# TensorE's opening: ten idle matmuls become 100 small ones in 64x64 quadrants and five of the old kind

## The chip, the cores and the metric

The kernel runs on one core of one Trainium2 chip. The metric is device time in microseconds for one launch, which takes `q`, `k`, `v`, `moe_w_in` and `moe_w_out` in float32 and returns one float32 array.

The engines that matter are TensorE (PE, with its weight loads shown apart as PEld), VectorE (DVE), ScalarE (ACT), GpSimd (POOL) and the sync engine (SP). DMA transfers are issued from the queues of POOL, SP and ACT.

## The reference

Windowed attention, then a feed-forward layer with a squared ReLU:

```python
# q, k, v: (8, 8, 576, 64); window = 32, dilation = 4
scores = scale * np.matmul(q, k.transpose(0, 1, 3, 2))
mask_plain = (rel >= 0) & (rel < window)                                   # heads 0 to 3
mask_dil = (rel >= 0) & (rel < window * dilation) & (rel % dilation == 0)  # heads 4 to 7
attn = softmax(np.where(masks, scores, -1e9))
x = np.matmul(attn, v).transpose(0, 2, 1, 3).reshape(4608, 512)
out = np.square(np.maximum(x @ w_in, 0.0)) @ w_out                         # w_in 512 x 2048, w_out 2048 x 512
```

## The kernel before, in words

The 4608 tokens pass through the feed-forward layer in tiles of 256 or 512 tokens. Each tile first multiplies by `w_in` (line 937, 16 blocks of the hidden dimension times four slices of the model dimension), then ACT evicts with a ReLU (line 950), DVE squares (line 951), and a second series of matmuls multiplies by `w_out` (line 979). The attention of the eight batches is woven between these matmuls, and its results go to `xT`, the moving operand of line 937. Every engine executes its own list of instructions in order. The order is written out by hand: a string, `PROGRAM`, holds short codes, and its first stretch (up to the first `|`) is what happens before the first feed-forward group.

That first stretch is called the head here. It does batch 0's attention:

- `load_qk` (line 171) and `load_v` (lines 192 and 198) issue, from POOL's queue, the transfers of `q`, `k` and `v` from HBM into staging tiles (`qb`, `kb`, `vd`, `vbd`). The same queue then issues `w_in` (line 1050) and `w_out` (line 1055).
- Codes `T` (line 761) transpose `q` and `k` on TensorE, as 64x64 or 80x64 pieces, into a PSUM tile `pa`; codes `C` (lines 768 to 776) copy them out.
- Codes `B` (line 791) put a mask's bias into PSUM, `S` (line 813) adds the scores in 64x64 quadrants, `E` (line 821) takes the exponential, `P` and `D` (lines 851 and 867) multiply by `v` and by ones, and `L`, `X` and `M` (lines 874, 877 and 884) divide.
- Codes `w` and `W` call `turn` (line 731): so many matmuls of a zero tile `idle` against itself. Their result is used by nobody. `w10` in front of the first transposes is ten of them with 512 columns; later `w1` and `W1` (256 columns) stand single between the steps. They write the PSUM tile `po`.

The tile `idle` is a part of `kbd` and is set to zero by a DVE memset (line 1001), which the first idle matmul waits for.

The PSUM pools of `po` and `pd` have one buffer each. Apart from idle matmuls their first users in the head are the `P` and `D` steps of heads 4 and 5 (code `P20`, at 12.18 us in the profile).

```python
PROGRAM = "... L1:q00123 z y L1:v0dp L1:q10123 w10 T00 C00a T10 C10a B00 B10 w1 S00 E00 ..."
```

## Time and profile before

| what | value |
|---|---|
| time, median of 3 | 299.54 us (299.31 to 303.17) |
| the profiled execution's own time | 299.32 us |
| its span, first to last instruction | 297.5 us |
| PE busy | 290.4 us, 3159 matmuls |
| ACT busy | 192.0 us |
| DVE busy | 168.0 us |
| POOL busy | 127.6 us |
| bytes moved by DMA | 35.37 MB |

The span ends 1.8 us short of the execution's own time; that rest lies outside the program's instructions. Times in the profile are counted from the span's start. A matmul's end is modelled, since matmuls overlap in the array: how fast TensorE goes is read from the distance between two starts. "Idle before" is the time in which an engine did nothing ahead of an instruction, with what ended it.

### The profile page before, as it was taken

How to read it: one execution, taken by the hardware profiler on the slowest of the kernel's cores; microseconds unless marked ns; L12 is line 12 of the kernel's file. 1: busy time of each engine (PE TensorE's matmuls, PEld its weight loads, DVE VectorE, ACT ScalarE, POOL GpSimd, SP SyncE). 2: the span in 40 equal slices, each digit the busy share in tenths (PEclk: the TensorE clock that was granted, in tenths of full speed). 3: DMA queues.
4: the chain of work that ended last, by engine and by line, in shares of the span. 5: the costliest groups of instructions: out<-in, count | busy, mean ns of one | idle time of the engine just before them, and what ended most of it. 6: DMA issues, size and time to landing. Idle time of an engine off the chain costs nothing.

```text
span 297.5 us, 7852 instructions
## 1 busy us (share of the span) xinstructions
PE 290.4 (98%) x3159; PEld 166.3 (56%) x3159; DVE 168.0 (56%) x508; ACT 192.0 (65%) x397; POOL 127.6 (43%) x208
## 2 busy tenths in 40 slices
PE   7899999999999999999999999999999999999994
PEld 3589657868755554555455445545554555445443
DVE  2776566967868665686749474957445234004400
ACT  6888568757958665888667667766676567127411
POOL 8579882676584383955783688100000000000000
PEclk9999999999999999999999999999999999999999
DMA  8999999999989999999999499112101200121022
GB/s 126 197 183 215 203 157 223 186 151 169 193 114 185 184 121 190 153 125 175 159 191 151 65 160 186 13 37 73 35 2 36 74 35 0 35 73 35 0 56 88
DMA packets 83124, 35.37 MB, mean 119 GB/s; under 512 B 52624, under 2 KB 78480, under 8 KB 83088
## 3 DMA queue, kind: packets, MB, share of 16 engines
q0 software_dynamic: 48992, 18.40, 54.8%
q1 hardware_dynamic: 33952, 16.38, 27.7%
q8 instruction: 25, 0.41, 0.6%
q10 hardware_dynamic: 144, 0.10, 0.1%
q14 instruction: 11, 0.09, 0.1%
HBM read 37.31 MB, written 9.44 MB: 157 GB/s over the span
## 4 chain that ended last, share of the span: by engine, by line
PE 90%; DMA 5%; ACT 2%; POOL 1%; issue 1%; DVE 1%; ACTq 0%; POOLq 0%
PE pf L937 42%; PE pf L979 40%; DMA w_in<-in_moe_w_in_dram 3%; DMA kb<-in_k_dram 2%; PE po L661 2%; PE pa L661 1%; PE pf L661 1%; POOL qb L171 1%; PE pa L277 1%; PE pd L661 1%; ACT rec L684 0%; ACT pt L698 0%; POOL kb L171 0%; ACT rec L674 0%; PE po L414 0%
## 5 line engine op out<-in xcount | busy, mean ns | idle before, releaser
L937 PE MATMUL pf<-xT,w_in 128*128 128x512 bf16 (+1 forms) x704 | 128.3, 341 | 1.3 <-DMA w_in<-in_moe_w_in_dram 1.3
L979 PE MATMUL pf<-w_out_sb,h2T 128*128 128x512 bf16 (+2 forms) x592 | 129.3, 374 | 0.0
L937 PEld LDWEIGHTS <-w_in 128*128 128x128 bf16 x704 | 77.9, 113 | 48.0 <-DMA w_in<-in_moe_w_in_dram 1.7
L950 ACT ACTIVATE h2T<-pf 128x512 bf16<-128x512 f32 x144 | 83.7, 600 | 29.5 <-PE pf L937 29.3
L951 DVE TENSOR_TENSOR h2T<-h2T 128x512 bf16<-128x512 bf16 x144 | 60.3, 424 | 60.1 <-ACT h2T L950 57.8
L979 PEld LDWEIGHTS <-h2T 128*128 128x128 bf16 x592 | 55.5, 98 | 61.6
L478 POOL DMA_DIRECT2D vbd<-in_v_dram x80 | 43.0, 547 | 24.3 <-DMA qb<-in_q_dram 10.2
L985 ACT COPY osb<-pf 128x512 f32<-128x512 f32 (+1 forms) x34 | 19.5, 573 | 49.7 <-PE pf L979 49.5
L171 POOL DMA_DIRECT2D qb<-in_q_dram x18 | 13.0, 720 | 9.7 <-DMA xx<-qb 7.9
L684 ACT ACTIVATE rec<-rec 128x576 f32<-128x576 f32 x24 | 16.4, 682 | 0.7
L698 ACT ACTIVATE pt<-pa 128x384 bf16<-128x384 f32 (+1 forms) x28 | 12.7, 498 | 6.2 <-DVE xT L689 3.7
L192 POOL DMA_DIRECT2D vbd<-in_v_dram x16 | 10.9, 691 | 9.1 <-DMA kb<-in_k_dram 4.3
L687 DVE TENSOR_TENSOR xT<-po,rec 128x512 bf16<-128x512 f32 x14 | 9.7, 691 | 7.5 <-ACT rec L684 7.2
L171 POOL DMA_DIRECT2D kb<-in_k_dram x18 | 12.7, 706 | 1.7 <-issue 0.7
L465 POOL DMA_DIRECT2D vd<-in_v_dram x20 | 12.0, 616 | 2.9 <-DMA vbd<-in_v_dram 2.9
L470 POOL DMA_DIRECT2D vbd<-in_v_dram x20 | 12.0, 615 | 2.7 <-DMA vbd<-in_v_dram 2.2
L700 DVE TENSOR_TENSOR pt<-pt,mask_n 128x448 bf16<-128x448 bf16 (+1 forms) x20 | 7.1, 373 | 9.5 <-ACT pt L698 9.4
L700 DVE TENSOR_TENSOR pt<-pt,mask_f 128x384 bf16<-128x384 bf16 x24 | 8.4, 355 | 6.0 <-ACT pt L698 5.9
L687 DVE TENSOR_TENSOR xT<-pf,rec 128x512 bf16<-128x512 f32 x10 | 6.9, 691 | 8.5 <-ACT rec L684 8.5
L492 DVE COPY qT<-xx 64x576 bf16<-64x576 bf16 (+1 forms) x30 | 10.8, 360 | 0.6
L661 PEld LDWEIGHTS <-vbd 64*64 64x64 bf16 x288 | 7.6, 107 | 4.2 <-issue 4.2
L698 ACT ACTIVATE pt<-pf 128x448 bf16<-128x448 f32 (+1 forms) x18 | 8.5, 521 | 0.5 <-PE pf L661 0.3
(156 smaller groups left out, 311.8 us busy)
## 6 DMA issues: line engine op xcount, KB each, us to landing
qb<-in_q_dram POOLq DMA_DIRECT2D x7, 320.0 KB, 5.3
kb<-in_k_dram POOLq DMA_DIRECT2D x7, 320.0 KB
vd<-in_v_dram POOLq DMA_DIRECT2D x32, 64.0 KB, 6.1
w_in<-in_moe_w_in_dram POOLq DMA_DIRECT2D x4, 512.0 KB, 8.6
w_out_sb<-in_moe_w_out_dram POOLq DMA_DIRECT2D x4, 512.0 KB, 13.0
out_dram<-osb SPq DMA_DIRECT2D x16, 128.0 KB, 5.3
qb<-in_q_dram POOLq DMA_DIRECT2D x7, 256.0 KB, 7.6
kb<-in_k_dram POOLq DMA_DIRECT2D x7, 256.0 KB
```

The source lines that it names most:

```text
L171: nc.gpsimd.dma_start(t[0:n, part, hs, :], src[b, hs, t0 : t0 + RES * n, :].rearrange("h (p r) d -> p h (r d)", r=RES))
L478: nc.gpsimd.dma_start(v_rows[b % 2][p0 + 16 * r : p0 + 16 * r + 16, e, :, :], v[b, 2 * e + hl, :, :].rearrange("(i m r) d -> r m i d", r=R ...
L661: nc.tensor.matmul(out, lhs, rhs, start=begin, stop=True, skip_group_check=True)
L684: nc.scalar.activation(rec[:, :], rec[:, :], ACT.Exp, scale=-1.0)
L687: nc.vector.tensor_tensor(out=tok[:, :, 16:M], in0=byr(o[:, :]), in1=byr(rec[:, 0:512]), op=ALU.mult)
L698: nc.scalar.activation(pt, sp[b, e][g][:, 0:n], ACT.Exp, scale=SCALE)
L700: nc.vector.tensor_tensor(out=pt, in0=pt, in1=mask, op=ALU.mult)
L937: nc.tensor.matmul(to, w_in_sb[piece][:, kt, c0 : c0 + 509 : 4], rhs, start=(kt == kts[0] and x == 0), stop=(kt == kts[-1] and x == per - ...
L950: nc.scalar.activation(hv, acc[u][:, :].rearrange("p (x n) -> p x n", x=per), ACT.Relu)
L951: nc.vector.tensor_tensor(out=hv, in0=hv, in1=hv, op=ALU.mult)
L979: nc.tensor.matmul(cur[m][:, c0:c1], h2[:, f, P * m : P * m + P], w_out_sb[:, f, c0:c1], start=(f == 0), stop=(f == NF - 1),)
L985: (nc.vector.tensor_copy if last and part == 1 or tk0 == 3 * NT // 2 else nc.scalar.copy)(osb[:, c0:c1], cur[m][:, c0:c1])
```

## The change

`w10` is replaced by `s100 w5`. The new code `s` calls `small_turns`, which issues 100 matmuls of 64 rows by 64 weight columns against 64 moving columns. They go round the four 64x64 quadrants of the array: the row half alternates with every matmul, the column half with every second one. Matmuls of the upper row half write `po`, those of the lower row half write `pd`. Each has its own weight load. The five idle matmuls of 512 columns that are kept follow and write the same `po`.

```diff
-    "L1:q00123 z y L1:v0dp L1:q10123 w10 T00 C00a T10 C10a B00 B10 w1 S00 E00 B20 W1 S10 E10 N u B30 W1 w1 T20q "
+    "L1:q00123 z y L1:v0dp L1:q10123 s100 w5 T00 C00a T10 C10a B00 B10 w1 S00 E00 B20 W1 S10 E10 N u B30 W1 w1 T20q "
...
+    def small_turns(n: int):
+
+        to = ps_o.tile([P, 512], f32, name="po"), ps_d.tile([P, 512], f32, name="pd")
+        first["W"] = to[0]
+        for x in range(n):
+            rows, cols = sides[x % 2], sides[x // 2 % 2]
+            nc.tensor.matmul(
+                to[x % 2][cols, 0:64], idle[rows, rows], idle[rows, 0:64], start=True, stop=True, skip_group_check=True
+            )
+
...
+        elif code[0] == "s":
+            small_turns(int(code[1:]))
```

## The prediction

> **What bounds the kernel now.** I read the page first: does TensorE bound the whole, and does its clock ever drop?

> ```profile
> span 297.5 us, 7852 instructions
> ...
> PE 290.4 (98%) x3159; PEld 166.3 (56%) x3159; DVE 168.0 (56%) x508; ACT 192.0 (65%) x397; POOL 127.6 (43%) x208
> ...
> PEclk9999999999999999999999999999999999999999
> ```

> TensorE is busy for 98% of the span. The change, however, touches only its first 3.5 us, so the view that decides is the chain of work over the first 30 us.

> ```profile
> 1.25 0.76 POOL qb L171
> ...
> 4.44 6.35 DMA kb<-in_k_dram
> 10.79 0.28 issue
> 11.07 8.43 DMA w_in<-in_moe_w_in_dram
> 19.51 0.05 issue
> 19.55 2.81 PE pf L937 x24
> ```

> No TensorE row stands in this chain before 19.55 us. Until then the end is set by POOL issuing transfers, by a `kb` transfer that frees POOL's queue, and by the `w_in` transfer that lands at 19.5 us. TensorE's own rows show how much room it has (the last bracket is idle time and what ended it):

> ```profile
> 1.07 3.69 PE L731 MATMUL po<-kbd 128*128 128x512 bf16 x10 [1.07 <-DVE kbd L1001]
> 4.74 0.31 PE L761 MATMUL pa<-mk,qb 64*64 64x64 bf16 x8
> 5.68 0.31 PE L761 MATMUL pa<-mk,kb 64*64 64x64 bf16 x8 [0.63 <-DMA kb<-in_k_dram]
> ...
> 15.02 1.94 PE L937 MATMUL pf<-xT,w_in 128*128 128x256 bf16 x16 [1.03 <-DMA w_in<-in_moe_w_in_dram]
> ...
> 19.55 0.63 PE L937 MATMUL pf<-xT,w_in 128*128 128x256 bf16 x4 [0.22 <-DMA w_in<-in_moe_w_in_dram]
> ```

> There are three waits for data that no TensorE instruction moves: at 5.68, 15.02 and 19.55 us. A delay of the opening is swallowed in turn by 0.63, 1.03 and 0.22 us of idle time.

> The page's clock row shows the full clock from the first slice on, and it misleads here. The weight loads of the ten idle matmuls tell their starts:

> ```profile
> 1.47 0.15 PEld L731 LDWEIGHTS <-kbd 128*128 128x128 bf16 x1 [0.28 <-issue]
> ...
> 3.18 0.15 PEld L731 LDWEIGHTS <-kbd 128*128 128x128 bf16 x1 [0.28 <-issue]
> 3.60 0.15 PEld L731 LDWEIGHTS <-kbd 128*128 128x128 bf16 x1 [0.28 <-issue]
> 3.95 0.31 PEld L731 LDWEIGHTS <-kbd 128*128 128x128 bf16 x2 [0.20 <-issue]
> ```

> From 1.47 to 3.60 us five steps take 2.13 us: 0.427 us for 512 columns, 1.2 columns per ns. The step from 3.60 to 3.95 is shorter (0.35), and the last two matmuls start 0.215 us apart, at 4.17 and 4.38 us in the timeline of shorter windows: 2.4 columns per ns. So TensorE starts at half speed and reaches full speed at about 3.86 us (0.35 us for 512 columns is 0.27 us at 1.2 and 0.08 at 2.4), that is after 2.8 us of unbroken matmuls. What the opening is good for, if anything, is this step.

> **The change, part by part.**

> *Removed:* five matmuls of 512 columns. At half speed each takes 0.427 us: 5 x 0.427 = 2.13 us of the opening.

> *Added:* 100 matmuls of 64 columns with a weight load each. The trace of before has the same form at full speed only. In the score and value steps of line 661 all four quadrants are in use, with about 82 columns per matmul:

> ```profile
> core 0: us, PE busy (x) PEld busy (x), PEclk, DMA share, GB/s
> ...
> 161.93:163.00 1.07, 1.07 (x108) 1.07 (x108) 1.00 1.54 134
> ```

> That is 108 in 1.07 us, 9.9 ns each, or 7.7 ns for 64 columns. Lower end, four quadrants side by side: at half speed 2 x 7.7 = 15.5 ns, 100 take 1.55 us. A nearer form in size, line 851's 16 matmuls of 64x64 in two quadrants at a time, start within 0.25 us (12.18 to 12.43): 16 ns each at full speed, 32 ns at half; 100 take 3.2 us. Upper end, one after the other: 64 columns at 1.2 per ns are 53 ns, 5.3 us at half speed. I take 1.55 us, since the order of the new matmuls goes round all four quadrants as in line 661.

> *Kept:* five matmuls of 512 columns. With 1.55 us the small ones end at 1.07 + 1.55 = 2.62. Two of the large ones take 0.427 each, to 3.47. The third runs into full speed at 3.86 and ends at 3.88, the last two take 0.215 each: the opening ends at 4.31 us, against 4.38 + 0.215 = 4.60 before. If full speed does not come by then, it ends at 2.62 + 2.13 = 4.75.

> *On the path:* nothing. The `qb` transfer lets TensorE start at 4.74 and the `kb` transfer at 5.68. The eight `qb` transposes take 0.12 us of starts, so the opening may last until 5.5 us before anything moves. With two quadrants at a time it would be: small ones by 4.27 at the latest, five large ones at full speed 1.08 more, 5.35 us. Also inside. An opening that ends earlier gains nothing either, since the transfers do not depend on it.

> *The other queues:* `po` and `pd` are first written by other work at 12.18 us, by TensorE itself, so the earlier use of `pd` adds no wait. No other engine's instructions change, nor DMA issues. TensorE's list grows by 2 x 95 = 190 instructions, less than one of the page's instruction packets (25 of 0.41 MB in all, 16 KB each), but all later packets are asked for earlier in the work. What hides them is the stock already fetched. Ends: a packet moves in 1.0 us (one in the slice at 12 us, 6.1% of 16 engines), so a fully exposed one loses 1.0 us; the longest wait of TensorE after 20 us is 0.2 us, so no more than that is to be gained. I take 0.

> Sum against the profiled execution: 297.5 + 1.8 + 0 = 299.3 us. The median of the runs shown is 0.2 us higher, 299.5, and I forecast that. About 2% (6 us) is what a measurement of this kernel can tell from no change.

> [...]

> **The rivals.**

> *1. Half speed stays (slower).* Small matmuls in quadrants fill less of the array at a time, and if they do not keep it busy enough, the step to full speed is missed at 3.86 us. For it: the mechanism was never tried with such matmuls in this trace, and the head after 4.74 is broken into short pieces. Against it: four quadrants together fill the array, five large matmuls follow, and the head has nine more idle ones. A short miss is free: the 1.03 us before 15.02 swallows it. It decides from the point where more than 1.03 us of full-speed matmul time has been stretched to twice its length. Price: the 214 matmuls of the head have 8.51 us of busy time with modelled ends. By the ratio of a 512-column matmul (0.215 of distance to 0.38 of busy) that is an estimated 4.8 us of array time. At half speed all the way to 15.02: +4.8 - 1.03 = +3.8 us, 303.1 to 303.3. If the first 16 matmuls of line 937 (1.94 us) run at half speed too: +1.7 - 0.22 more, 304.8. Were all 8.51 us stretched, it is over 306. I take 303.2.

> *2. The quadrants do not overlap (the change doesn't do what it says).* 100 at 53 ns until 3.86 us are 52, the other 48 at 27 ns take 1.3: 5.16, and with 1.08 for the large ones 6.2 us. That is 0.7 late, less than 1.03: 299.5. Without the step to full speed: 1.07 + 5.3 + 2.13 = 8.5, late by 3.0; less 1.03 and 0.22 it costs 1.8 us: 301.3.

> *3. A little faster.* Fetches that fall in better places, or an opening whose end at 4.31 frees something unseen: by the waits above at most 0.2 at 19.55 and some tenths later: 298.7.

> **How the numbers follow.** No change, within 0.6 us of 299.5: 0.76. Rival 1: 0.11, of which 0.04 over 305.5 us, the bound of 2%. Rival 2 with a cost: 0.04. Rival 3: 0.07. What is left, 0.02, is unnamed and small. The range from 298.4 to 303.6 leaves out about half of rival 1 and little else; its long side is rival 1's lower price. Faster by over 2% would be below 293.5 us: the trace has not that much idle time on TensorE. Faster 0.01, same 0.95, slower 0.04.

> **What would show it.** Right: about 100 matmuls of 64x64 in front of five large ones, ending near 4.3 us; starts 0.215 us apart among the last large ones; still a wait of about 1 us for `w_in` before 15.0 us and the chain on `w_in` until 19.5. Wrong by rival 1: idle matmuls of the head 0.427 us apart, and that wait gone. Wrong by rival 2: the transposes of `kb` start after 5.7 us, with no wait for their transfer. The forecast falls if TensorE's first matmul of line 937 starts later than 15.1 us, or if the part after 19.55 us takes longer than 278 us.

## The result, and the profile after

The changed kernel is slower: 304.10 us as the median of 21 runs (301.35 to 311.33), against 299.54 us before (298.70 to 303.17). The ratio is 1.0104, with a 95% interval of 1.0079 to 1.0129: a loss under the 2% that the prediction names as what can be told from no change, but with an interval clear of 1. This ratio compares only runs within 1.5% of the fastest one of their kernel; since the cause found below also spreads a kernel's runs, the median and range of all runs stand beside each ratio. The profiled execution took 302.65 us, 3.33 us more than before's 299.32.

The page after, in the parts shown before:

```profile
span 300.9 us, 8042 instructions
...
PE 294.1 (98%) x3254; PEld 169.3 (56%) x3254; DVE 167.5 (56%) x508; ACT 191.8 (64%) x397; POOL 128.1 (43%) x208
...
PEclk9589999999999999999999999999999999999999
```

What is new is in the clock row: in the second and third slices of 7.5 us full speed is missing. Windows of the span show the loss with its edges. The columns are the window, its length, busy time and count of PE, PEld, DVE, ACT and POOL, then the granted clock, the DMA share and GB/s. After:

```profile
4.20:7.61 3.41, 1.74 (x39) 0.99 (x37) 0.28 (x1) 1.39 (x5) 3.41 (x6) 1.00 1.22 172
7.61:17.85 10.24, 10.22 (x154) 6.33 (x155) 5.54 (x16) 5.22 (x14) 7.40 (x12) 0.50 1.35 197
17.85:30.00 12.15, 11.98 (x203) 10.89 (x200) 9.21 (x24) 10.93 (x25) 10.78 (x11) 1.00 1.24 207
```

Before:

```profile
3.86:7.27 3.41, 2.73 (x50) 1.49 (x49) 0.79 (x3) 1.73 (x5) 3.41 (x6) 1.00 1.31 186
7.27:17.85 10.58, 9.48 (x225) 6.94 (x226) 7.88 (x23) 8.14 (x20) 6.98 (x11) 1.00 1.38 197
```

Full speed begins at 4.20 us (3.86 before), lasts 3.41 us and is then lost for 10.24 us, three times as long. In the window before the loss TensorE is busy for 1.74 us, before it was 2.73. TensorE's timeline says why (lines are ten further down than before, so 761 is 771 here):

```profile
2.31 0.24 PE L741 MATMUL po<-kbd 64*64 64x64 bf16 x1
2.32 0.24 PE L741 MATMUL pd<-kbd 64*64 64x64 bf16 x1
2.32 0.24 PE L741 MATMUL po<-kbd 64*64 64x64 bf16 x1
2.32 0.24 PE L741 MATMUL pd<-kbd 64*64 64x64 bf16 x1
2.36 0.24 PE L741 MATMUL po<-kbd 64*64 64x64 bf16 x1
...
2.55 2.05 PE L731 MATMUL po<-kbd 128*128 128x512 bf16 x5
4.67 0.31 PE L771 MATMUL pa<-mk,qb 64*64 64x64 bf16 x8
6.58 0.31 PE L771 MATMUL pa<-mk,kb 64*64 64x64 bf16 x8 [1.60 <-DMA kb<-in_k_dram]
...
10.54 0.61 PE L731 MATMUL po<-kbd 128*128 128x512 bf16 x1
```

The small matmuls do go four abreast, a turn every 53 ns (64 columns at 1.2 per ns). But the transposes of `kb` start at 6.58 us instead of 5.68, after 1.60 us of waiting. At 10.54 an idle matmul shows 0.61 us busy, where one at full speed showed 0.38.

The transfer queues tell what delayed `kb`. Between 3.8 and 5.4 us the changed kernel has a line that before's trace lacks there:

```profile
q8 instruction: 1, 0.02, 4.1%
```

It is one packet of 16 KB, from 4.23 us on, 1.04 us long on one DMA engine. I take q8 for the queue of TensorE's instruction list: before, it moves 25 such packets while TensorE goes through 6318 weight loads and matmuls, some 253 each. The first `kb` transfer takes 4.5 us from issue to landing:

```profile
DMA to landing us min/median/max: 4.5/4.5/4.5
```

It lands in 16 parts. By the trace's landing marks 15 of them were there by 5.65 us and the last at 6.53; before, 5.56 and 5.63.

The chain of work over the first 30 us, which had no TensorE row before 19.55 us, is TensorE's now:

```profile
2.01 4.52 DMA kb<-in_k_dram
6.53 0.04 issue
6.58 0.56 PE pa L771 x24
7.14 0.41 PE pf L801 x4
...
13.93 1.21 PE pa L771 x32
15.14 0.70 PE pf L861 x8
...
19.65 1.03 PE pf L947 x8
```

In the profiled execution all the lost time lies in the head. The seventeenth matmul of line 937 (947 after), the one that waited for `w_in` at 19.55 us, starts at 22.98, 3.43 us later. From it to the span's end it takes 277.90 us, before 277.99.

### The profile page after: what moved, and what is told of

Its sections match the earlier page's. It is cut to its first block, busy times and chain, and to the rows that moved or that the text cites. A ratio compares the mean times of both kernels' runs of the same rounds, so it can differ in the third digit from the quotient of the medians.

```text
span 300.9 us, 8042 instructions
## 1 busy us (share of the span) xinstructions
PE 294.1 (98%) x3254; PEld 169.3 (56%) x3254; DVE 167.5 (56%) x508; ACT 191.8 (64%) x397; POOL 128.1 (43%) x208
## 4 chain that ended last, share of the span: by engine, by line
PE 93%; ACT 2%; DMA 2%; issue 1%; DVE 1%; POOL 0%; ACTq 0%; POOLq 0%
PE pf L989 42%; PE pf L947 40%; PE po L661 2%; DMA kb<-in_k_dram 2%; PE pf L661 1%; PE pa L661 1%; PE pa L771 1%; PE po L731 1%; ACT rec L884 1%; ACT rec L887 1%; PE pd L661 1%; PE pa L277 1%; DVE xT L894 1%; PE pf L823 1%; ACT h2T L960 0%
## 5 line engine op out<-in xcount | busy, mean ns | idle before, releaser
L995 ACT COPY osb<-pf 128x512 f32<-128x512 f32 (+1 forms) x34 | 19.5, 574 | 49.7 <-PE pf L989 46.6
L171 POOL DMA_DIRECT2D qb<-in_q_dram x18 | 13.0, 721 | 14.1 <-DMA xx<-qb 12.1
L698 ACT ACTIVATE pt<-pa 128x384 bf16<-128x384 f32 (+1 forms) x28 | 12.7, 498 | 6.1 <-DVE xT L689 3.6
L171 POOL DMA_DIRECT2D kb<-in_k_dram x18 | 12.7, 704 | 1.7 <-issue 0.7
```

Of the source, the lines that this page charges most:

```text
L171: nc.gpsimd.dma_start(t[0:n, part, hs, :], src[b, hs, t0 : t0 + RES * n, :].rearrange("h (p r) d -> p h (r d)", r=RES))
L698: nc.scalar.activation(pt, sp[b, e][g][:, 0:n], ACT.Exp, scale=SCALE)
L995: (nc.vector.tensor_copy if last and part == 1 or tk0 == 3 * NT // 2 else nc.scalar.copy)(osb[:, c0:c1], cur[m][:, c0:c1])
```

## The experiments

Three theories stood at first. T: the opening is too short; in the changed kernel it is 1.3 + 2.1 us at half speed, before it was 4.3. F: 190 more instructions bring the packet beside the `kb` transfer, and the wait that follows loses full speed. A: matmuls in quadrants count for little or nothing as activity. All kernels compute the whole result. Each edit replaces `s100 w5` of the changed kernel, in some with other sizes in `small_turns`.

| kernel | opening, at half speed | list against before | median, us (range, runs) | before beside it | ratio (95% interval) | last part of first `kb` lands |
|---|---|---|---|---|---|---|
| w8 | 3.4 us | -4 | 301.47 (298.51 to 307.99, 10) | 299.81 | 1.0011 (0.9979 to 1.0043) | 5.65 |
| w5 | 2.1 | -10 | 303.33 (299.96 to 305.49, 9) | 299.50 | 1.0104 (1.0071 to 1.0137) | 5.33 |
| q20w5 | 2.1 + 2.1 | +30 | 299.54 (298.99 to 300.18, 10) | 299.81 | 0.9995 (0.9982 to 1.0007) | 5.34 |
| q40 | 4.3, all in quadrants | +60 | 299.32 (298.98 to 299.58, 10) | 299.64 | 0.9995 (0.9976 to 1.0015) | 5.83 |
| q12w5 | 1.3 + 2.1 | +14 | 301.83 (299.60 to 304.37, 10) | 299.57 | 1.0059 (1.0027 to 1.0090) | 5.42 |
| q12w7 | 1.3 + 3.0 | +18 | 299.84 (299.27 to 302.09, 10) | 299.57 | 1.0019 (0.9993 to 1.0045) | 5.49 |
| s60w6 | 0.8 + 2.6 | +112 | 301.39 (299.88 to 305.02, 10) | 299.81 | 1.0046 (1.0016 to 1.0076) | 5.45 |
| s50x128 | 1.3 + 2.1 | +90 | 303.10 (301.33 to 306.47, 4) | 299.50 | 1.0103 (1.0058 to 1.0147) | 5.40 |
| s50x128w7 | 1.3 + 3.0 | +94 | 302.36 (300.75 to 304.30, 10) | 299.64 | 1.0097 (1.0063 to 1.0130) | 5.55 |
| s50x128w10 | 1.3 + 4.3 | +100 | 300.86 (299.56 to 301.86, 10) | 299.64 | 1.0043 (1.0019 to 1.0067) | 5.50 |
| s100w7 | 1.3 + 3.0 | +194 | 303.07 (299.77 to 310.68, 10) | 299.50 | 1.0073 (1.0041 to 1.0104) | 6.90 |
| s100w10 | 1.3 + 4.3 | +200 | 300.33 (299.32 to 301.79, 10) | 299.81 | 1.0025 (1.0004 to 1.0046) | 6.89 |
| split | 1.3 + 2.1, six more after `q` | +202 | 300.35 (299.80 to 301.74, 10) | 299.50 | 1.0031 (1.0015 to 1.0048) | 6.92 |
| after2, the change again | 1.3 + 2.1 | +190 | 303.57 (303.22 to 309.35, 4) | 299.57 | 1.0134 (1.0085 to 1.0183) | 6.97 |

**A shorter opening of the old kind: w8 and w5.**

```diff
-s100 w5
+w8
```

> Eight idle matmuls of 512 columns in place of ten: the opening ends near 4.2 us, as early as in the changed kernel (4.43 us), with no small matmul and no more instructions than before. Theory F (the longer instruction list makes TensorE fetch its next 16 KB packet at 4.2 us, beside the kb transfer, which then lands 0.9 us late; TensorE idles 1.8 us, falls to half speed at the end of a 3.4 us window): kb transposes at 5.7 us, full speed kept, 299.5 us (299.0 to 300.2). Theory A (matmuls in quadrants count for too little activity): the same, 299.5. Theory T (the opening is too short): half speed in the head, 302 or more.

```diff
-s100 w5
+w5
```

> Five large idle matmuls and no small ones: the opening is 2.1 us long at half speed. Theory T: full speed is missed or lost more often than with w8 (301.5 us), 303 to 306 us. Theory A: the same time as with the 50 or 100 small ones in front of them. If the small ones count as time, this kernel is slower than s50x128 by 1 us or more.

Theory T has the sign right. With eight matmuls the median of 301.47 us is a little under the 302 that T expected. The ratio shows no difference, but four of the ten runs lie at 303.6 us or more, where the 31 of before beside them end at 300.63. With five, seven of nine runs lie between 302.9 and 305.5. In w5's profile full speed comes only at 10.0 us; that profile is of its fastest run, 299.96 us, so what the runs of 303 us lost stands in no trace. The mean granted clock of all nine is 0.998 or more, so it is not a loss that the clock records. The length of the opening matters, then, and eight matmuls are already too few.

**Quadrants for as long as the large ones took: q20w5 and q40.**

```diff
-                to[x % 2][cols, 0:64], idle[rows, rows], idle[rows, 0:64], start=True, stop=True, skip_group_check=True
+                to[x % 2][cols, 0:512], idle[rows, rows], rhs, start=True, stop=True, skip_group_check=True
...
-s100 w5
+s20 w5
```

> 20 quadrant matmuls of 512 columns (5 turns round the four quadrants, 2.13 us at half speed) and five of the old kind: as much time in quadrants as the removed matmuls took, but only 30 instructions more than before, so that the packet is not fetched beside the kb transfer. Theory F: kb transposes at 5.7 us, full speed kept, 299.5 us (299.0 to 300.3). Theory A: full speed comes late or is lost, 301.5 to 306 us.

q20w5 is as fast as before, but its five large matmuls now run up to 5.5 us, next to the transposes; that would help even if the quadrants counted for nothing. So q40 leaves the large ones out:

```diff
-s20 w5
+s40
```

> 40 quadrant matmuls of 512 columns and no large ones: 4.3 us at half speed, as long as before's opening, all of it in quadrants. If quadrants count as busy time like large matmuls: 299.5 us (299.0 to 300.3). If they count for half or less: full speed comes only with the head's own work, 301.5 to 305 us.

It is as fast as before, and no run is above 299.58 us. Theory A falls: a window that quadrants alone filled, from 1.73 to 5.14 us, was followed by full speed. The small ones of 64 columns count too. In the changed kernel the window before 4.20 us, which brought full speed, is filled to 0.88, and the large matmuls from 2.55 us on are only 0.48 of it; the table further down has windows with 0.55 and 0.66 that brought none. Whether a quadrant counts in full is not shown: by the 0.65 of that table, about two thirds would have done in q40.

**The packet away from `kb`: s60w6.**

```diff
-s100 w5
+s60 w6
```

> 60 small matmuls and six large ones: the opening ends near 4.3 us as in the changed kernel, 60% of the small matmuls stay, but the packet that was fetched after 212 weight loads and matmuls is now asked for after the kb transposes have begun. Theory F: kb transposes at 5.7 us, full speed kept, 299.5 us (299.0 to 300.5). Theory A: slower by more than half of what the change costs, 301 to 305 us.

`kb` lands at 5.45 us, as F expects, and a part of the loss remains. But the profile puts little of it in the head: the seventeenth matmul of line 947 starts at 19.69 us, 0.14 later than before's. The part after it takes 279.07 us, 1.08 more than before's, with a wait that neither theory expected, at 73.75 us; it is taken up below. So this run does not tell T from F.

**The packet beside `kb`, with a longer opening: s100w10 and s100w7.**

```diff
-s100 w5
+s100 w10
```

> All 100 small matmuls and all ten large ones: the opening ends near 5.4 us, the packet is fetched near 4.2 us as in the changed kernel. Theory F: the kb transposes start near 6.5 us again, but TensorE idles only 1.0 us before them, so full speed is likely kept: the price of the late kb transfer by itself, 299.5 to 300.5 us, since 1.0 us of waiting for w_in before 15 us swallows it. Theory A: as many large matmuls as before, full speed kept, kb transposes at 5.7 us, 299.5 us.

```diff
-s100 w5
+s100 w7
```

> All 100 small matmuls and seven large ones: 4.4 us at half speed, as long as before's 4.3, with the packet fetched near 4.2 us and kb late. Theory T: 299.7 to 300.5 us. Theory F: kb is late, and after the opening at full speed TensorE idles over 1 us, so some runs lose full speed: 300.5 to 303. Theory A: as w7 alone, between w8 (301.5) and w5, 302 or more.

In both the packet comes at 4.0 to 4.4 us, and the last part of `kb` lands at 6.9. s100w10's opening lasts until 6.6 us, so TensorE does not wait for `kb`, and with it late the kernel costs 0.25%. s100w7, with an opening as long as before's, loses full speed as the changed kernel did, one window after it came (5.37 to 8.78 us), for 10.24 us. Its profiled run is one of its longer ones, 307.35 us.

**The wait filled: split.**

```diff
-s100 w5 T00 C00a
+s100 w5 T00q w6 T00k C00a
```

> The changed kernel with six more large idle matmuls between the transposes of q and those of k, where TensorE waited for the late kb transfer (1.8 us in the profile). The packet is still fetched at 4.2 us and kb stays late. If the loss comes from the idle time that follows the opening (theories T and F), full speed is kept: 299.5 to 300.7 us, with the kb transposes near 6.6 us. Theory A, that the opening itself is what fails: 302 us or more.

This is the changed kernel with its late `kb`, and its six large matmuls fill what was a wait:

```profile
4.52 0.31 PE L771 MATMUL pa<-mk,qb 64*64 64x64 bf16 x8
4.76 1.47 PE L731 MATMUL po<-kbd 128*128 128x512 bf16 x6
6.96 0.31 PE L771 MATMUL pa<-mk,kb 64*64 64x64 bf16 x8 [0.73 <-DMA kb<-in_k_dram]
```

It takes 300.35 us, 0.85 over before: most of the loss is gone, though `kb` is as late as ever. The clock agrees in every run: the mean granted clock of split's ten runs is 0.997 or more, while nine of the changed kernel's 21 have 0.976 to 0.983, and 0.983 is what 10.24 us at half speed make of its span. The loss comes through the idle time behind the opening.

**The opening's length kept, the list shortened: s50x128, s50x128w7, s50x128w10.**

```diff
-                to[x % 2][cols, 0:64], idle[rows, rows], idle[rows, 0:64], start=True, stop=True, skip_group_check=True
+                to[x % 2][cols, 0:128], idle[rows, rows], idle[rows, 0:128], start=True, stop=True, skip_group_check=True
...
-s100 w5
+s50 w5
```

> 50 quadrant matmuls of 128 columns instead of 100 of 64, then five large ones: the opening is as long as in the changed kernel (1.3 us in quadrants, 2.1 us in large ones at half speed), but with 100 instructions fewer, so the packet is fetched after the first kb transfer has landed. Theory T (what counts is the length of the opening at half speed, 4.3 us before, 3.6 now): as w8, whose opening is 3.4 us, 301 to 302 us. Theory F (the packet makes kb late, and the long idle loses full speed): nearer to before than w8, 299.5 to 300.8. Theory A (quadrants count for nothing): as w5.

The other two differ from it by `w7` and `w10`:

> 50 quadrant matmuls of 128 columns and seven large ones: the opening of s100w7 (1.3 us in quadrants, 3.0 us in large ones at half speed) with 100 instructions fewer, so the packet no longer meets the kb transfer. If the late kb is what costs s100w7 its 3.5 us: kb transposes before 5.8 us, 299.5 to 300.5 us. If quadrants in the opening are the cause: 302 to 304 us again.

> The opening of s100w10 (300.3 us) without the late kb. If the late kb costs something even where full speed is kept: 299.5 us, 0.5 to 1 us under s100w10. If not: 300.3 us, as s100w10.

These three were meant to take F out and did not. `kb` lands on time in all, but new waits stand late in their traces, in which TensorE waits for nothing that the profile shows. The list of waits of s50x128:

```profile
PE pf L989 <- issue: 1.5, 1, 1.5
...
PE pf L947 <- issue: 0.6, 1, 0.6
```

(The numbers are the waits' total in us, their count and the longest.) They end at 75.4 and 81.6 us. s50x128w7 has one of 1.6 us at 81.0, s50x128w10 one of 1.0 us at 79.4, s60w6 one of 0.9 us at 73.8:

```profile
73.75 0.38 PE L947 MATMUL pf<-xT,w_in 128*128 128x256 bf16 x2 [0.92 <-issue]
```

In these four kernels the part from the seventeenth matmul of line 937 to the end takes 279.1 to 280.2 us; in before, the changed kernel and q40 it takes 277.9 to 278.0. All four lists are 90 to 112 longer than before's. That a packet of the list comes too late is the likely reason, and the traces point to it in two ways. Each of the five waits ends 1.3 to 1.7 us after a packet of q8 has moved. And the long wait stands before the same instruction in all three s50x128 kernels, the 2227th weight load or matmul by order of start, although the work there differs (line 989 in one, two places of line 661 in the others); the other wait of s50x128 stands 255 instructions earlier, about one packet. So it belongs to a place in the list, not to a step of the work. No kernel tried it by itself. It means that s50x128w7 cannot be held against s100w7.

**The same openings with hardly a longer list: q12w5, q12w7, and the change again.**

```diff
-                to[x % 2][cols, 0:64], idle[rows, rows], idle[rows, 0:64], start=True, stop=True, skip_group_check=True
+                to[x % 2][cols, 0:512], idle[rows, rows], rhs, start=True, stop=True, skip_group_check=True
...
-s100 w5
+s12 w5
```

> 12 quadrant matmuls of 512 columns (1.3 us at half speed) and five large ones: the changed kernel's opening in length and kind, with 14 instructions more than before instead of 190. If the shorter opening is the whole cause: 303 to 304 us, as the changed kernel. If the packet beside kb is the whole cause: 299.5 us, kb transposes at 5.7 us. If both: as w8, 300.5 to 302 us.

> 12 quadrant matmuls of 512 columns and seven large ones: as long as before's opening (4.3 us at half speed) and as that of s100w7 (303.1 us), without the packet beside kb and without the stall at 74 to 82 us. Length decides: 299.5 us (299.0 to 300.3), which leaves the 3.5 us of s100w7 to its longer list.

> The changed kernel once more, beside the other two: kb transposes at 6.4 us or later, with the packet fetched near 4.2 us; full speed lost in the head, or reached late; 303 to 305 us.

q12w7 (`s12 w7`) is within 0.2% of before. Its twin with the longer list, s100w7, took 303.07 us: 3.2 us more by the medians, 0.5% by the ratios. q12w5, the changed kernel's opening with hardly a longer list, costs 0.59%. The changed kernel beside it costs 1.34%, 1.04% in its first runs. By these ratios the shorter opening has about half of the loss, and the longer list the other half: 0.45 to 0.75%, 1.3 to 2.2 us. With intervals of 0.25 to 0.5% to either side this split is rough.

It is also less clean than it looks, since both kernels still wait for nothing that the profile shows, q12w7 until 14.76 us and q12w5 until 15.80:

```profile
PE pf L824 <- issue: 1.4, 1, 1.4
...
PE pf L824 <- issue: 1.6, 1, 1.6
```

Both waits stand before the 447th weight load or matmul, as does one of 0.5 us in q40, and end 1.35 and 1.51 us after a packet of q8 has moved: the list again, it seems, whose first packet moves at 11 to 13 us in these kernels. So q12w5's profiled run, 300.50 us, which keeps full speed from 5.28 us on and has the first part of `w_in` at 14.43, lost its time in such a wait and not by the clock; five of its ten runs have a mean granted clock of 0.983 to 0.994.

The repeat shows the same course as the first profile:

```profile
4.80 0.42 PE L771 MATMUL pa<-mk,qb 64*64 64x64 bf16 x8
7.01 0.31 PE L771 MATMUL pa<-mk,kb 64*64 64x64 bf16 x8 [1.80 <-DMA kb<-in_k_dram]
```

Its windows:

```profile
5.34:8.75 3.41, 1.69 (x39) 1.13 (x39) 0.93 (x3) 0.76 (x3) 2.46 (x5) 1.00 1.23 158
8.75:18.99 10.24, 10.24 (x168) 6.73 (x167) 5.61 (x16) 6.11 (x16) 7.28 (x11) 0.50 1.39 192
```

| kernel, window in us | with transposes | without | speed after it |
|---|---|---|---|
| before, 0.44 to 3.86 | 0.82 | 0.82 | full |
| w8, 2.09 to 5.50 | 0.76 | 0.69 | full |
| s50x128, 2.86 to 6.27 | 0.81 | 0.55 | half |
| after, 4.20 to 7.61 | 0.36 | 0.22 | half (lost) |
| after, 7.61 to 11.02 | 0.72 | 0.66 | half |
| after, 11.02 to 14.44 | 0.79 | 0.43 | half |
| after, 14.44 to 17.85 | 0.79 | 0.65 | full |
| s100w7, 5.37 to 8.78 | 0.44 | 0.30 | half (lost) |
| q12w5, 8.69 to 12.10 | 0.55 | 0.27 | full (kept) |

With transposes counted no threshold fits: 0.81 stays at half speed and 0.76 goes to full. Without them one at 0.65 does, to within a hundredth, in all 16 traces: each window that was followed by full speed has 0.65 or more, each that left TensorE at half speed 0.66 or less. A threshold for losing full speed lies much lower, near 0.3, and is less sharp: q12w5 kept it at 0.27, s100w7 lost it at 0.30. The step of 3.41 us is in every trace (10.24 is three of them); that transposes do not count like other matmuls is this table's reading alone, and no kernel here tried it by itself. Less than a whole window was enough: 0.65 of it, 2.2 us.

## Why the prediction was wrong, point by point

- *What bounds the kernel.* Right for before: its chain runs over `w_in`. But the idle time of 0.63, 1.03 and 0.22 us was taken for granted as room, and it holds only if `kb` is on time and the clock at full speed. That the wait until 15.02 us was for `w_in` is not certain either: by the landing marks its last part was there at 14.84, and the wait stands before the 447th weight load or matmul, where q12w5, q12w7 and q40 wait for nothing that the profile shows.
- *Removed and added.* Near enough. The small ones take 1.31 us from 1.07 us on, 0.24 less than the 1.55 taken, because four run abreast at the full 13.3 ns each; the large ones follow after a further 0.17 us at 2.55, and the opening ends at 4.43 us, against 4.31 predicted.
- *The other queues.* Here the failure lies. The step "I take 0" priced the packet at 0 to 1.0 us as a stall of TensorE's list. It never stalled the list in the changed kernel's profiled head. It moved from 12.7 to 4.2 us and took 1.04 us of one DMA engine, and one sixteenth of `kb` came late: 0.9 us, in the repeat 1.3. All five traces with a packet at 3.9 to 4.4 us have `kb` complete at 6.5 to 7.0 us, the eleven others at 5.3 to 5.8. That the late part is the one that shares the packet's engine is inferred from this; the traces do not name the engines. That instructions already fetched hide a packet holds in before's trace: 26 matmuls and 25 weight loads are at work while its second one moves (17.75 to 18.72 us), and after 20 us, where 23 packets move, TensorE's longest wait is 0.2 us. If the waits for nothing that the profile shows are the list's, it did not hold everywhere, and the bound of 1.0 us was too low as well: single waits took 1.4 to 1.6 us, and s50x128 lost 2.1 us in two.
- *On the path: nothing.* "The transfers do not depend on it" was wrong for that reason. The step also took an opening that ends earlier for harmless; the idle time behind it cost the clock here (1.60 us of waiting, then 10.24 us at half speed).
- *Rival 1.* Its price was right (303.2, the profiled execution has 302.65, the median 304.1), its place too: the head at half speed. Its reason was wrong: a window filled by quadrants alone was enough (q40). Full speed came, at 4.20 us, and was lost a window later. That the price fits is in part luck: it was worked out for half speed up to 15.02 us without a break, and what came was full speed from 4.20 to 7.61 us, 1.60 us of it idle, and half speed until 17.85. With the loss of cover counted, the chance of 0.11 was far too low, and the upper end of 303.6 too.
- *Rival 2.* Refuted: 53 ns for a turn of four.
- *What would show it.* Of the signs named for a fall, line 937's first matmul later than 15.1 us came true (18.56 us), and the part after the head kept within 278 us.
- *The sum.* 3.43 us in the head, where 0 was written, and -0.09 us behind it. By the ratios, roughly half of the loss comes from the shorter opening (0.59% in q12w5) and half from the longer list.

What stays open: why some runs of the changed kernel go up to 311 us. By the mean granted clock nine of the 21 lost three windows or more (0.976 to 0.983; 302.65 to 307.17 us) and nine about one (0.991 to 0.994), but of these four took 301.35 to 302.12 us and five 308.14 to 311.33. Only one run per kernel has a trace. s100w7's profile has a second loss, at 77.1 us after a wait of 2.4 us for DVE; it lasted one window, 3.41 us.

## What to carry to other kernels

Idle matmuls at the start bought full clock in these traces only where they, and the work that followed, filled enough of one window (0.65 of 3.41 us, transposes left out). Its phase can't be counted on: the first change of the clock fell anywhere between 3.8 and 10.0 us. So choose their length for the worst phase, and let them reach the first real work. Count time, not matmuls: four quadrants abreast did as well as the whole array in q40 (299.32 us, before 299.64). Added instructions are not free because their engine is idle: here 190 of them moved each of the list's 25 fetches ahead in the work, by 14 to 372 weight loads and matmuls, and a fetch can hold back the data that the engine waits for, as the one at 4.23 us did with `kb` (0.9 us).

## What was not expected of the hardware

- With one packet of 16 KB of instructions beside it, the last sixteenth of a 128 KB transfer landed 0.9 to 1.5 us after the fifteenth, and with it the whole, in five traces of five.
- TensorE's full speed, once lost, stayed away for exactly 10.24 us, three windows, in all three traces where it was lost in the head, while TensorE looked busy for 10.22 of 10.24 us in the first of them. It is not a fixed time: s100w7's second loss lasted 3.41 us.
- In before the granted clock reads 1.00 until its first change is recorded, at 3.86 us, while 512 columns take 0.427 us up to 3.60; the row does not show the slow start.
